# Placing the start of a long-convolution kernel by hand: Sin order, a small add, a copy, and the loads of q

## The chip, the cores and the metric

The kernel runs on one core of a Trainium2 chip. The metric is device time in microseconds (us) of one execution. Each comparison below was timed in five rounds on one chip, against fresh runs of the kernel before.

Engines are named as in the profile: PE is TensorE (matmul), DVE is VectorE, ACT is ScalarE, POOL is GpSimd, and SP is the engine whose queue issues most loads. A letter L with a number is a line of that kernel's own source, so the same statement has different numbers in different kernels.

## The reference

Shortened; only the middle lines of `_A_ref` are put in words. Shapes are 2048 rows by 576 channels, bfloat16. The program has two layers, but the reference multiplies the layernorm of x by a convolution of k and v, which does not depend on x, so the kernel computes the convolution once.

```python
def _A_ref(q, k, v, shift_k, ssm_k, ssm_D):            # q is layernorm(x)
    k_shift = sum over t of k_pad[:, t:t+S, :] * shift_k[:, ks-1-t]     # 4 taps
    kv = k_shift * v
    y = irfft(rfft(kv, zero-padded) * rfft(ssm_k, zero-padded))[:S]      # long convolution
    y = y + kv * ssm_D
    return q * y

x = A_q
x = x + _A_ref(_layernorm(x), A_k, A_v, A_shift_k, A_ssm_k, A_ssm_D)
x = x + (gelu(n @ w_gate) * (n @ w_up)) @ w_down       # n = layernorm(x)
# ... and both once more with the same inputs: the second layer
```

## The kernel before

The convolution is done by blocks of 512 rows with matrices instead of an FFT. GF is the forward transform matrix and GI the inverse one. Both are generated on the core: VectorE computes an integer angle (`j`, then `jm`), and ScalarE takes its Sin.

```python
def emit(dst, col_ap_halves, row_scalar, offs):
    j = work.tile([P, NDFT], I32, tag="dft_j", bufs=2)
    ...
    jm = work.tile([P, NDFT], I32, tag="dft_jm", bufs=3)
    nc.vector.tensor_single_scalar(out=jm[:, 0:W], in_=j[:, 0:W], scalar=N4 - 1, op=ALU.bitwise_and)
    nc.scalar.activation(out=dst, in_=jm[:, 0:W], func=ACT.Sin, bias=negpi[:], scale=sc)

for kt in range(KT_F):        # 4 pieces of GF, 128x1024
    emit(GF[:, kt, :], ...)
for kt in range(KT_I):        # 8 pieces of GI, 128x512
    emit(GI[:, kt, :], ...)
```

Then come the loads: `skb` (the four taps), `hn` (the filter, four blocks), `dvec` (ssm_D), then k and v, the first feed-forward weights, and 16 tiles of q for layernorm statistics. ScalarE rearranges the taps: `nc.scalar.copy(out=skc, in_=skb rearranged)`.

The filter blocks are transposed, copied and transformed:

```python
def fwd(src_blk, d0, dw, scale, dst):                  # 32 matmuls of dw columns, 4 evacuations
    for mt0 in range(0, MT, MP):
        ps = psT.tile([P, MP, 512], F32, tag="psT")
        ...  nc.tensor.matmul(ps[:, mi, 0:dw], lhsT=GF[...], rhs=src_blk[:, kt, d0:d0 + dw], ...)
        nc.scalar.activation(out=dst[:, mt0:mt0 + MP, :], in_=ps[:, :, 0:dw], func=ACT.Copy, scale=scale)

for blk in range(NBLK):
    hT_blk = kvp.tile([P, STB, D], BF16, tag="hT_blk")
    ...  # 20 transposes by TensorE; two ScalarE copies PSUM -> hT_blk
    if blk == 0:
        nc.vector.tensor_tensor(out=hT_blk[0:1, 0, :], in0=hT_blk[0:1, 0, :], in1=dvec[:], op=ALU.add)
    for pi in porder:                                  # 64 columns ("thin"), then 512 ("wide")
        fwd(hT_blk, d0, dw, 2.0 / NDFT, Hf[(pi, blk)])
```

An evacuation is the `activation` in `fwd`: ScalarE copies finished sums from TensorE's result buffer (`ps`) into `dst`. The same `fwd` then transforms the four kv blocks, which VectorE prepares in eight groups of multiplications and adds ("kv groups"). After that VectorE multiplies the spectra (`pr`), TensorE sums the products (`Yps`) and applies GI. From about 216 us on the feed-forward part runs, which the change does not touch.

The order of instructions on each engine is fixed when the kernel is built, by a scheduler. In the traces here an engine whose next instruction waits does not take a later one: in skb_first, below, TensorE stood 5.67 us before one matmul with 40 others behind it.

## Time and profile before

| | before |
|---|---|
| time, median of 6 runs before the prediction | 1144.62 us (1141.97 to 1147.25) |
| profiled run: time and span | 1143.58 us, 1141.8 us |
| first filter transform on TensorE | 20.52 us |
| first kv transform | 69.48 us |
| first feed-forward matmul | 215.55 us |
| feed-forward part | 926.3 us |

The page of before, parts 1 and 4: busy time of each engine, and the chain of work that ended last, by engine.

```profile
PE 1077.9 (94%) x6340; PEld 519.8 (46%) x6464; DVE 487.3 (43%) x1023; ACT 296.1 (26%) x481; POOL 47.6 (4%) x96
...
PE 82%; DVE 11%; issue 4%; ACT 2%; POOL 1%; DMA 1%; SPq 0%; DVEq 0%; POOLq 0%
```

TensorE is the limit of the whole. So a change to the other engines is worth only what it removes from TensorE's waits. The longest stands at the start. In the timeline view each line gives the start, the duration, engine, source line, operation, output<-input, shapes and count; in square brackets is how long the engine had been idle and what released it. First before's TensorE:

```profile
6.96 2.89 PE L256 MATMUL pt<-ident,hn 128*128 128x128 bf16 x20 [6.96 <-DMA hn<-in_A_ssm_k_dram]
20.52 1.01 PE L184 MATMUL ps<-hT_blk,GF 128*128 128x64 bf16 x16 [10.68 <-DVE hT_blk L260]
...
31.42 0.98 PE L256 MATMUL pt<-ident,hn 128*128 128x128 bf16 x10
```

TensorE has its transposes done at 9.85 us and then sits idle for 10.68 us. The name behind the arrow is the small `dvec` add on VectorE. The timelines of before's ScalarE and VectorE say why it is so late:

```profile
5.36 2.30 ACT L164 COPY skc<-skb 128x2304 bf16<-128x2304 bf16 x1 [3.34 <-DMA skb<-in_A_shift_k_dram]
...
9.61 1.28 ACT L58 ACT_TABLE_LOAD   x1
10.90 1.15 ACT L58 ACTIVATE GF<-jm,negpi 128x1024 bf16<-128x1024 int32 x1
11.96 1.10 ACT L258 COPY hT_blk<-pt 128x1152 bf16<-128x1152 bf16 x1
12.96 3.23 ACT L58 ACTIVATE GF<-jm,negpi 128x1024 bf16<-128x1024 int32 x3
16.09 4.51 ACT L58 ACTIVATE GI<-jm,negpi 128x512 bf16<-128x512 int32 x7
```

```profile
12.09 0.69 DVE L57 TENSOR_SCALAR jm<-j 128x1024 int32<-128x1024 int32 x1 [4.33 <-ACT GF L58]
...
19.94 0.43 DVE L260 TENSOR_TENSOR hT_blk<-hT_blk,dvec 1x576 bf16<-1x576 bf16 x1
...
22.00 0.76 DVE L274 TENSOR_TENSOR acc<-kj,skc 128x1152 bf16<-128x1152 bf16 x1 [1.22 <-DMA kj<-in_A_k_dram]
```

ScalarE's first large instruction waits for the load of the taps; behind it come a copy of `hT` (1.12 us) and the load of the Sin table (1.28 us), so the first Sin starts at 10.90 us. VectorE has only three `jm` buffers, so it waits for Sins too (4.33 us). And the add stands behind nearly all of GI's angles, though TensorE needs only GF.

### The profile page before, as it was taken

Reading aid. Unit: us, or ns where it says so; the run is one execution under the profiler, and the core shown is the slowest. Engines: PE = TensorE matmul, PEld = TensorE weight load, DVE = VectorE, ACT = ScalarE, POOL = GpSimd, SP = SyncE. Lnnn points to the kernel's source line nnn. Section 1 sums busy time; section 2 is a strip of 40 time slices with the busy share of each in tenths; the row PEclk is TensorE's granted clock in tenths of the full one; section 3 lists DMA queues with packets and bytes.
Section 4 is the critical chain, followed back from the end, with each engine's and each line's share of the span. In section 5 each row is a group of like instructions: output and inputs, shape, how many; then the busy total and the mean of one; then the engine's idle time right before and its main releaser. Section 6 shows DMA issues by size and latency. Waiting matters only on the chain.

```text
span 1141.8 us, 15444 instructions
## 1 busy us (share of the span) xinstructions
PE 1077.9 (94%) x6340; PEld 519.8 (46%) x6464; DVE 487.3 (43%) x1023; ACT 296.1 (26%) x481; POOL 47.6 (4%) x96
## 2 busy tenths in 40 slices
PE   3889888699999999999999999999999999999997
PEld 2444333344444444444444444444444444444443
DVE  6966789822256224932353236323222322232222
ACT  6555320511113111331113111311131111111111
POOL 0010000200001000200010001000000000000000
PEclk9999999899999999999999999999999999999999
DMA  8932000980000000000000000000000000000000
GB/s 248 289 99 72 1 1 3 354 265 1 1 1 1 1 1 1 1 1 1 1 1 1 1 1 1 1 1 21 1 1 1 21 1 1 1 22 1 1 1 21
DMA packets 35957, 41.09 MB, mean 36 GB/s; under 512 B 2101, under 2 KB 33712, under 8 KB 35888
## 3 DMA queue, kind: packets, MB, share of 16 engines
q1 hardware_dynamic: 33776, 35.39, 10.1%
q0 software_dynamic: 2112, 4.72, 1.5%
q8 instruction: 50, 0.82, 0.3%
q14 instruction: 19, 0.16, 0.0%
HBM read 35.38 MB, written 2.36 MB: 33 GB/s over the span
## 4 chain that ended last, share of the span: by engine, by line
PE 82%; DVE 11%; issue 4%; ACT 2%; POOL 1%; DMA 1%; SPq 0%; DVEq 0%; POOLq 0%
PE pg L506 20%; PE pu L506 20%; PE acc L523 19%; PE pu L509 5%; PE pg L509 5%; PE ps L184 4%; PE acc L526 3%; DVE pr L219 3%; PE ps L244 2%; POOL rstd L302 1%; DVE stats L298 1%; DVE x_c L315 1%; PE Yps L223 1%; PE pt L460 1%; DVE hT L517 1%
## 5 line engine op out<-in xcount | busy, mean ns | idle before, releaser
L517 DVE TENSOR_TENSOR hT<-ga,pu 128x512 bf16<-128x512 f32 x288 | 197.4, 685 | 575.8 <-PE pu L509 567.9
L515 ACT ACTIVATE ga<-pg 128x512 f32<-128x512 f32 x288 | 171.6, 596 | 685.1 <-PE pg L509 644.4
L523 PE MATMUL acc<-wd,hT 128*128 128x512 bf16 x1101 | 312.3, 380 | 2.1 <-DVE hT L517 2.1
L506 PE MATMUL pg<-xnT,wg 128*128 128x512 bf16 x1132 | 294.2, 380 | 1.2 <-issue 0.2
L506 PE MATMUL pu<-xnT,wu 128*128 128x512 bf16 x1128 | 291.6, 379 | 2.0 <-ACT ga L515 1.0
L526 PE MATMUL acc<-wd,hT 128*128 128x64 bf16 x1152 | 222.0, 193 | 2.5
L523 PEld LDWEIGHTS <-hT 128*128 128x128 bf16 x1152 | 112.7, 98 | 138.8 <-DVE hT L517 5.7
L506 PEld LDWEIGHTS <-wu 128*128 128x128 bf16 x1152 | 112.8, 98 | 137.5 <-issue 2.1
L506 PEld LDWEIGHTS <-wg 128*128 128x128 bf16 x1152 | 93.7, 98 | 102.6 <-issue 0.5
L526 PEld LDWEIGHTS <-hT 128*128 128x128 bf16 x1152 | 112.9, 98 | 32.4
L509 PE MATMUL pu<-xnT_rB,wr 128*128 128x512 bf16 x288 | 109.2, 379 | 0.9
L509 PE MATMUL pg<-xnT_rA,wr 128*128 128x512 bf16 x276 | 104.8, 380 | 0.0
L509 PEld LDWEIGHTS <-wr 128*128 128x128 bf16 x576 | 56.4, 98 | 68.1 <-issue 0.3
L219 DVE TENSOR_TENSOR pr<-KVf,Hf 128x128 bf16<-128x128 bf16 (+1 forms) x160 | 64.0, 451 | 33.3 <-PE Yps L223 16.2
L184 PEld LDWEIGHTS <-GF 128*128 128x128 bf16 x512 | 36.6, 104 | 52.4 <-issue 14.0
L184 PE MATMUL ps<-hT_blk,GF 128*128 128x64 bf16 (+1 forms) x252 | 38.6, 313 | 14.9 <-DVE hT_blk L260 10.7
L302 POOL TENSOR_TENSOR rstd<-ve,neghalf_t 128x1 f32<-128x1 f32 x48 | 35.7, 744 | 357.1 <-DVE ve L301 340.3
L223 PE MATMUL Yps<-pr,ident 128*128 128x512 bf16 (+1 forms) x176 | 44.8, 331 | 1.6 <-DVE zb L233 0.6
L298 DVE BATCH_NORM_STATS2 stats<-x_c 128x6 f32<-128x288 f32 x96 | 40.3, 437 | 0.0
L244 PE MATMUL ps<-zb,GI 128*128 128x64 bf16 (+1 forms) x190 | 29.2, 285 | 10.4 <-DVE zb L236 6.8
L440 ACT ACTIVATE xn<-x_c,nbias,rstd 128x576 bf16<-128x576 f32 x32 | 27.5, 860 | 34.9 <-DVE nbias L437 18.3
L184 PE MATMUL ps<-kv_blk,GF 128*128 128x64 bf16 (+1 forms) x253 | 32.8, 285 | 3.4 <-ACT KVf L187 1.4
(71 smaller groups left out, 449.0 us busy)
## 6 DMA issues: line engine op xcount, KB each, us to landing
kj<-in_A_k_dram SPq DMA_DIRECT2D x29, 288.0 KB, 4.3
wd<-in_B_w_down_dram SPq DMA_DIRECT2D x9, 576.0 KB, 7.2
wg<-in_B_w_gate_dram SPq DMA_DIRECT2D x9, 512.0 KB, 8.2
wu<-in_B_w_up_dram SPq DMA_DIRECT2D x9, 512.0 KB, 9.8
x_c<-in_A_q_dram POOLq DMA_DIRECT2D x4, 1152.0 KB, 7.0
v_t<-in_A_v_dram SPq DMA_DIRECT2D x8, 288.0 KB, 3.6
qt<-in_A_q_dram SPq DMA_DIRECT2D x16, 144.0 KB, 3.0
out_dram<-ob SPq DMA_DIRECT2D x16, 144.0 KB, 1.7
```

Source lines behind the costliest of these rows:

```text
L184: nc.tensor.matmul(ps[:, mi, 0:dw], lhsT=GF[:, kt, mt * P:(mt + 1) * P], rhs=src_blk[:, kt, d0:d0 + dw], start=(kt == 0), stop=(kt == KT_F ...
L219: nc.vector.tensor_tensor(out=pr[:], in0=kvf[:, ko:ko + HH, :], in1=hf[:, ho:ho + HH, :], op=ALU.mult)
L223: nc.tensor.matmul(Yflat[:, c0:c0 + cw], lhsT=idm[:], rhs=prf[:, c0:c0 + cw], start=(ti == 0), stop=(ti == n_terms - 1))
L244: nc.tensor.matmul(ps[:, mi, 0:dw], lhsT=GI[:, kt, mt * P:(mt + 1) * P], rhs=zb[:, kt, :], start=(kt == 0), stop=(kt == KT_I - 1))
L298: nc.vector.bn_stats(out=stats[:, h, :], in_=x_ap[:, h * w:(h + 1) * w])
L302: nc.gpsimd.tensor_tensor(out=rstd_out, in0=ve[:], in1=neghalf_t[:, 0:1], op=ALU.pow)
L506: nc.tensor.matmul(pd[:], lhsT=wm[:, dt, fi * P:(fi + 1) * P], rhs=xnT[:, dt, :], start=(dt == 0), stop=(dt == NDTF - 1 and not DREM))
L509: nc.tensor.matmul(pd[:], lhsT=wr[g][:, fi * P:(fi + 1) * P], rhs=rr[:], start=False, stop=True)
L515: nc.scalar.activation(out=ga[:], in_=pg[:], func=ACT.Gelu_apprx_tanh)
L517: nc.vector.tensor_tensor(out=hT[:], in0=ga[:], in1=pu[:], op=ALU.mult)
L523: nc.tensor.matmul(acc[:, j, 0:DM], lhsT=hT[:, j * P:(j + 1) * P], rhs=wd[g][:, fi, 0:DM], start=(f == 0), stop=(f == FT - 1))
L526: nc.tensor.matmul(acc[:, STC, j * DR:(j + 1) * DR], lhsT=hT[:, j * P:(j + 1) * P], rhs=wd[g][:, fi, DM:D], start=(f == 0 and j == 0), sto ...
```

## The change

The intent is to let TensorE's first transform start earlier, without new work. Most of it is ordering: dependencies that only the scheduler sees, and that add no wait on the chip. No arithmetic is added or removed.

- The four GF pieces go first on VectorE and ScalarE; the index row `colf` is made before the identity matrix on POOL.
- The `dvec` add goes before GI; the tap copy goes behind the four thin evacuations of block 0; the eight GI Sins go between wide evacuations (three in block 0, five in block 1).
- The q loads move from SP's queue to POOL's, with two buffers instead of three, and the q statistics come behind kv block 0.
- The first down-projection weight is loaded after the convolution part.

The core of the diff, with cuts marked by dots:

```diff
+        colf = tmpc.tile([P, NF], F32, name="colf")
+        nc.gpsimd.iota(colf[:], ...)          # before ident and rowf
+        if pre_cb is not None:
+            pre_cb()                          # make_identity
...
+    i_skc = nc.scalar.copy(out=skc[:], in_=skb[:].rearrange("p d j -> p j d"))
+    after(i_skc, "gf_last_sin", "DMA-fed rearrangement must not block the DFT matrix generation")
...
-            nc.scalar.copy(out=hT_blk[:, j0:j0 + MP, :], in_=pt[:, :, 0:D])
+            i_cp = nc.scalar.copy(out=hT_blk[:, j0:j0 + MP, :], in_=pt[:, :, 0:D])
+            if blk == 0:
+                after(i_cp, "gf_last_sin", "GF first on ScalarE")
         if blk == 0:
-            nc.vector.tensor_tensor(out=hT_blk[0:1, 0, :], ..., in1=dvec[:], op=ALU.add)
+            i_add = nc.vector.tensor_tensor(out=hT_blk[0:1, 0, :], ..., in1=dvec[:], op=ALU.add)
+            for i_gi in marks["gi_ands"]:
+                tc.add_manual_dep(i_gi.ins, i_add.ins.name, SCHED, reason="dvec add before GI")
...
+    sched(i_skc, evac[3], "skc behind the thin evacuations of block 0")
+    for i in range(8):
+        sched(marks["gi_sins"][i], evac[4 + i if i < 3 else 8 + i], "GI Sins between wide evacuations")
...
+                    if g == 0:
+                        after(i_first, "gf_last_and", "GF first on VectorE (kv ops wait on DMA)")
+                        tc.add_manual_dep(i_first.ins, i_add.ins.name, SCHED, reason="dvec add first")
+                        sched(i_first, marks["gi_ands"][2], "3 GI pieces before the kv ops")
...
+        if blk == 0 and early_cb is not None:
+            early_cb[1](ktmp, lambda inst: tc.add_manual_dep(inst.ins, i_kvlast.ins.name, SCHED,
+                                                             reason="q stats after kv block 0"))
...
-            qt = scratch.tile([P, D], BF16, tag="qtmp", bufs=3)
-            nc.sync.dma_start(out=qt[:], in_=q2[st * P:(st + 1) * P, :])
+            qt = scratch.tile([P, D], BF16, tag="qtmp", bufs=2)
+            nc.gpsimd.dma_start(out=qt[:], in_=q2[st * P:(st + 1) * P, :])
...
+    alloc_w(wpool, 0, gu=False)
+    load_w(0, gu=False)                       # wd of group 0, now behind the convolution part
```

More of the change, by code (lines that the diff above doesn't have):

```diff
@@ L21, with _gen_dft_mats @@
 NF = BS
-def _gen_dft_mats(tc, pool_gf, pool_gi, G_dtype, tmpc, work):
+def _gen_dft_mats(tc, pool_gf, pool_gi, G_dtype, tmpc, work, pre_cb=None):
     nc = tc.nc
@@ L30, in _gen_dft_mats @@
     GI = pool_gi.tile([P, KT_I, BS], G_dtype, name="GI")
+    marks = {}
     if True:
@@ L34, in _gen_dft_mats @@
                        allow_small_or_imprecise_dtypes=True)
+        colf = tmpc.tile([P, NF], F32, name="colf")
+        nc.gpsimd.iota(colf[:], pattern=[[2, NF]], base=1, channel_multiplier=0,
+                       allow_small_or_imprecise_dtypes=True)
+        if pre_cb is not None:
+            pre_cb()
         rowf = tmpc.tile([P, 2, KT_F], F32, name="rowf")
         nc.gpsimd.iota(rowf[:], pattern=[[0, 2], [2 * P, KT_F]], base=1, channel_multiplier=2,
-                       allow_small_or_imprecise_dtypes=True)
-        colf = tmpc.tile([P, NF], F32, name="colf")
-        nc.gpsimd.iota(colf[:], pattern=[[2, NF]], base=1, channel_multiplier=0,
                        allow_small_or_imprecise_dtypes=True)
@@ L56, in emit @@
             jm = work.tile([P, NDFT], I32, tag="dft_jm", bufs=3)
-            nc.vector.tensor_single_scalar(out=jm[:, 0:W], in_=j[:, 0:W], scalar=N4 - 1, op=ALU.bitwise_and)
-            nc.scalar.activation(out=dst, in_=jm[:, 0:W], func=ACT.Sin, bias=negpi[:], scale=sc)
+            i_and = nc.vector.tensor_single_scalar(out=jm[:, 0:W], in_=j[:, 0:W], scalar=N4 - 1, op=ALU.bitwise_and)
+            i_sin = nc.scalar.activation(out=dst, in_=jm[:, 0:W], func=ACT.Sin, bias=negpi[:], scale=sc)
+            return i_and, i_sin
         for kt in range(KT_F):
-            emit(GF[:, kt, :], [(colf[:], NF), (colf[:], NF)], rowv[:, kt:kt + 1],
-                 [3 * NDFT, 0])
+            i_and, i_sin = emit(GF[:, kt, :], [(colf[:], NF), (colf[:], NF)], rowv[:, kt:kt + 1],
+                                [3 * NDFT, 0])
+        marks["gf_last_and"] = i_and
+        marks["gf_last_sin"] = i_sin
         for kt in range(KT_I):
             off = 3 * NDFT if kt < KT_F else 0
-            emit(GI[:, kt, :], [(colt[:], BS)], rowf[:, kt // KT_F, kt % KT_F: kt % KT_F + 1], [off])
-    return GF, GI
+            i_and, i_sin = emit(GI[:, kt, :], [(colt[:], BS)], rowf[:, kt // KT_F, kt % KT_F: kt % KT_F + 1], [off])
+            marks.setdefault("gi_sins", []).append(i_sin)
+            marks.setdefault("gi_ands", []).append(i_and)
+        marks["gi_last_and"] = i_and
+        marks["gi_last_sin"] = i_sin
+    return GF, GI, marks
 @with_exitstack
 def ssm_phase_A(ctx, tc, y_sb, ident, A_k, A_v, A_shift_k, A_ssm_k, A_ssm_D, G_dtype=BF16,
-                after_loads_cb=None, early_cb=None):
+                after_loads_cb=None, early_cb=None, pre_cb=None):
     nc = tc.nc
@@ L110, in ssm_phase_A, with after @@
     dft_work = dft_es.enter_context(tc.tile_pool(name="dft_work", bufs=2))
-    GF, GI = _gen_dft_mats(tc, gfp, gip, G_dtype, dft_tmp, dft_work)
+    GF, GI, marks = _gen_dft_mats(tc, gfp, gip, G_dtype, dft_tmp, dft_work, pre_cb=pre_cb)
+    SCHED = mybir.DependencyInfo(mybir.DependencyClass.NoSync, mybir.DependencyReason.SCHED_ONLY)
+    def after(inst, mark, why):
+        tc.add_manual_dep(inst.ins, marks[mark].ins.name, SCHED, reason=why)
     hn = []
@@ L149, in ssm_phase_A @@
             else:
-                nc.vector.memset(kj[0:j, 0, :], 0.0)
+                i_ms = nc.vector.memset(kj[0:j, 0, :], 0.0)
+                after(i_ms, "gf_last_and", "GF first on VectorE")
                 nc.sync.dma_start(out=kj[j:P, 0, :], in_=k2[0:P - j, :])
@@ L157, in ssm_phase_A @@
         ksh_all.append((ksh, v_t))
-        if g == 1 and after_loads_cb is not None:
-            after_loads_cb()
-    if early_cb is not None:
-        early_cb(dft_work)
+        if g == 1:
+            if after_loads_cb is not None:
+                after_loads_cb()
+            if early_cb is not None:
+                early_cb[0](ktmp)
     dft_es.close()
-    nc.scalar.copy(out=skc[:], in_=skb[:].rearrange("p d j -> p j d"))
+    i_skc = nc.scalar.copy(out=skc[:], in_=skb[:].rearrange("p d j -> p j d"))
+    after(i_skc, "gf_last_sin", "DMA-fed rearrangement must not block the DFT matrix generation")
     sgn_i = gip.tile([P, 1], I32, name="sgn_i")
@@ L176, in ssm_phase_A @@
     MP = 2
+    evac = []
     def fwd(src_blk, d0, dw, scale, dst):
@@ L186, in fwd @@
                                      start=(kt == 0), stop=(kt == KT_F - 1))
-            nc.scalar.activation(out=dst[:, mt0:mt0 + MP, :], in_=ps[:, :, 0:dw], func=ACT.Copy, scale=scale)
+            evac.append(nc.scalar.activation(out=dst[:, mt0:mt0 + MP, :], in_=ps[:, :, 0:dw], func=ACT.Copy, scale=scale))
     ypool_cm = tc.tile_pool(name="A_Y", bufs=1)
@@ L257, in ssm_phase_A @@
                                         identity=ident[0:dsz, 0:dsz])
-            nc.scalar.copy(out=hT_blk[:, j0:j0 + MP, :], in_=pt[:, :, 0:D])
+            i_cp = nc.scalar.copy(out=hT_blk[:, j0:j0 + MP, :], in_=pt[:, :, 0:D])
+            if blk == 0:
+                after(i_cp, "gf_last_sin", "GF first on ScalarE")
         if blk == 0:
-            nc.vector.tensor_tensor(out=hT_blk[0:1, 0, :], in0=hT_blk[0:1, 0, :], in1=dvec[:], op=ALU.add)
+            i_add = nc.vector.tensor_tensor(out=hT_blk[0:1, 0, :], in0=hT_blk[0:1, 0, :], in1=dvec[:], op=ALU.add)
+            for i_gi in marks["gi_ands"]:
+                tc.add_manual_dep(i_gi.ins, i_add.ins.name, SCHED, reason="dvec add before GI")
         for pi in porder:
@@ L263, in ssm_phase_A, with sched @@
             fwd(hT_blk, d0, dw, 2.0 / NDFT, Hf[(pi, blk)])
+    def sched(a, b, why):
+        tc.add_manual_dep(a.ins, b.ins.name, SCHED, reason=why)
+    sched(i_skc, evac[3], "skc behind the thin evacuations of block 0")
+    for i in range(8):
+        sched(marks["gi_sins"][i], evac[4 + i if i < 3 else 8 + i], "GI Sins between wide evacuations")
     for blk in range(NBLK):
@@ L273, in ssm_phase_A @@
                 if idx == 0:
-                    nc.vector.tensor_tensor(out=acc[:], in0=ksh[j][:], in1=skj, op=ALU.mult)
+                    i_first = nc.vector.tensor_tensor(out=acc[:], in0=ksh[j][:], in1=skj, op=ALU.mult)
+                    if g == 0:
+                        after(i_first, "gf_last_and", "GF first on VectorE (kv ops wait on DMA)")
+                        tc.add_manual_dep(i_first.ins, i_add.ins.name, SCHED, reason="dvec add first")
+                        sched(i_first, marks["gi_ands"][2], "3 GI pieces before the kv ops")
                 else:
@@ L278, in ssm_phase_A @@
                     nc.vector.tensor_tensor(out=acc[:], in0=acc[:], in1=tmp[:], op=ALU.add)
-            nc.vector.tensor_tensor(out=kv_blk[:, gi * GST:(gi + 1) * GST, :], in0=acc[:], in1=v_t[:], op=ALU.mult)
+            i_kvlast = nc.vector.tensor_tensor(out=kv_blk[:, gi * GST:(gi + 1) * GST, :], in0=acc[:], in1=v_t[:],
+                                               op=ALU.mult)
+            if g == 0:
+                for i in range(3, 8):
+                    sched(marks["gi_ands"][i], i_kvlast, "rest of GI after kv group 0")
         for pi in porder:
@@ L346, in ssm_geglu_kernel @@
     ident = persist.tile([P, P], BF16, name="ident")
-    make_identity(nc, ident[:])
     eps_t = persist.tile([P, 1], F32, name="eps_t")
@@ L354, in ssm_geglu_kernel, with alloc_w @@
     fw = FG * P
-    def alloc_w(pool, g):
-        wg[g] = pool.tile([P, NDTF, fw], BF16, name=f"wg{g}")
-        wu[g] = pool.tile([P, NDTF, fw], BF16, name=f"wu{g}")
-        wr[g] = pool.tile([P, fw], BF16, name=f"wr{g}") if DREM else None
-        wd[g] = pool.tile([P, FG, D], BF16, name=f"wd{g}")
-    def load_w(g):
-        f0 = g * fw
-        nc.sync.dma_start(out=wg[g][:], in_=B_w_gate[0:NDTF * P, f0:f0 + fw].rearrange("(dt p) f -> p dt f", p=P))
-        nc.sync.dma_start(out=wu[g][:], in_=B_w_up[0:NDTF * P, f0:f0 + fw].rearrange("(dt p) f -> p dt f", p=P))
-        if DREM:
-            nc.sync.dma_start(out=wr[g][0:DREM, :], in_=B_w_gate[NDTF * P:D, f0:f0 + fw])
-            nc.sync.dma_start(out=wr[g][DREM:2 * DREM, :], in_=B_w_up[NDTF * P:D, f0:f0 + fw])
-        nc.sync.dma_start(out=wd[g][:], in_=B_w_down[f0:f0 + fw, :].rearrange("(ft p) d -> p ft d", p=P))
+    def alloc_w(pool, g, gu=True, dn=True):
+        if gu:
+            wg[g] = pool.tile([P, NDTF, fw], BF16, name=f"wg{g}")
+            wu[g] = pool.tile([P, NDTF, fw], BF16, name=f"wu{g}")
+            wr[g] = pool.tile([P, fw], BF16, name=f"wr{g}") if DREM else None
+        if dn:
+            wd[g] = pool.tile([P, FG, D], BF16, name=f"wd{g}")
@@ new lines, in load_w @@
+    def load_w(g, gu=True, dn=True):
+        f0 = g * fw
+        if gu:
+            nc.sync.dma_start(out=wg[g][:], in_=B_w_gate[0:NDTF * P, f0:f0 + fw].rearrange("(dt p) f -> p dt f", p=P))
+            nc.sync.dma_start(out=wu[g][:], in_=B_w_up[0:NDTF * P, f0:f0 + fw].rearrange("(dt p) f -> p dt f", p=P))
+            if DREM:
+                nc.sync.dma_start(out=wr[g][0:DREM, :], in_=B_w_gate[NDTF * P:D, f0:f0 + fw])
+                nc.sync.dma_start(out=wr[g][DREM:2 * DREM, :], in_=B_w_up[NDTF * P:D, f0:f0 + fw])
+        if dn:
+            nc.sync.dma_start(out=wd[g][:], in_=B_w_down[f0:f0 + fw, :].rearrange("(ft p) d -> p ft d", p=P))
@@ L371, in ssm_geglu_kernel, with q_loads @@
     pre = ctx.enter_context(tc.tile_pool(name="pre", bufs=1))
-    alloc_w(pre, 0)
+    alloc_w(pre, 0, dn=False)
     qmv = persist.tile([P, NST, 2], F32, name="qmv")
     qrstd = persist.tile([P, NST], F32, name="qrstd")
-    def q_stats(scratch):
+    q_tiles = []
+    def q_loads(scratch):
+        for st in range(NST):
+            qt = scratch.tile([P, D], BF16, tag="qtmp", bufs=2)
+            nc.gpsimd.dma_start(out=qt[:], in_=q2[st * P:(st + 1) * P, :])
+            q_tiles.append(qt)
@@ L378, in q_stats, with q_compute @@
+    def q_compute(scratch, after_fn):
         nchunk = 2 if D > nc.vector.BN_STATS_FMAX else 1
@@ L380, in q_stats @@
         for st in range(NST):
-            qt = scratch.tile([P, D], BF16, tag="qtmp", bufs=3)
-            nc.sync.dma_start(out=qt[:], in_=q2[st * P:(st + 1) * P, :])
+            qt = q_tiles[st]
             stats = scratch.tile([P, nchunk, nc.vector.BN_STATS_DIM], F32, tag="qstats", bufs=2)
             for h in range(nchunk):
-                nc.vector.bn_stats(out=stats[:, h, :], in_=qt[:, h * w:(h + 1) * w])
+                i_bn = nc.vector.bn_stats(out=stats[:, h, :], in_=qt[:, h * w:(h + 1) * w])
+                if h == 0:
+                    after_fn(i_bn)
             nc.vector.bn_aggr(out=qmv[:, st, :], in_=stats[:])
@@ L389, in q_stats @@
         nc.gpsimd.tensor_tensor(out=qrstd[:], in0=ve[:], in1=neghalf_t[:, 0:1].to_broadcast([P, NST]), op=ALU.pow)
-    ssm_phase_A(tc, y_sb, ident, A_k, A_v, A_shift_k, A_ssm_k, A_ssm_D, after_loads_cb=lambda: load_w(0),
-                early_cb=q_stats)
+    ssm_phase_A(tc, y_sb, ident, A_k, A_v, A_shift_k, A_ssm_k, A_ssm_D, after_loads_cb=lambda: load_w(0, dn=False),
+                early_cb=(q_loads, q_compute), pre_cb=lambda: make_identity(nc, ident[:]))
     if debug == "y":
```

## The prediction

> **What bounds the kernel now.** TensorE: the page has PE busy 94% of 1141.8 us, and the chain of waits is 82% PE. From 217 us on runs the feed-forward part, which the change does not touch. The change works on the first 110 us (making the DFT matrices GF and GI by Sin, block transforms of the filter, then of kv) and on when some loads are issued.
>
> **Where time is lost there.** In the timeline PE finishes its first transposes at 9.85 us and waits 10.7 us for the first transform (20.5). Its last releaser is the dvec add (19.94 us, 0.43 us), which stands behind nearly all of GI's generation on VectorE. Behind that: ScalarE waits until 5.36 us for the skb load, copies it (2.30 us), copies hT (1.12 us), and only then starts the Sins at 10.9 us.
>
> **What the change does.** No arithmetic goes. The four GF Sins (1.15 us each) go before everything fed by a load; the dvec add before GI; the eight GI Sins (0.72 us) between evacuations; the skb copy behind the thin evacuations. The q loads move from SP's queue to POOL's with two buffers instead of three, q statistics behind kv block 0, and the first down-projection weight is loaded after the SSM phase.
>
> **New start, from the trace's durations.** colf ready about 1.5 us; one GF piece each 1.4 us on VectorE; identity 2.5, then its negation and a table load (1.28) to about 4.2; four Sins end at about 8.7. The hn load (6.9 us) and transposes (9.85) now gate: hT copies end at about 11. dvec is issued near 4.7 us instead of 8.7, behind three hn blocks; at the 300 GB/s of the windows it lands near 10.5. Add 0.43: first transform at about 11.6 us, **8.9 us earlier**.
>
> **How much survives.** A wide evacuation (1.02 us) comes every 1.73 us, so one Sin just fits between two. The Sin behind block 1's last evacuation delays the next hT copies: −0.7 us. PE's cold stretch (half-rate spacing until 26.4 us) may shorten a little: the Trainium skill, "TensorE: Matmul & The Clock Gate", Part 1, describes warming after sustained activity; this trace shows about 6 us of it. VectorE must reach the first products by about 68 us on the new scale; summing its work I get 64, so 4 us of slack. q tiles through POOL (the skill's "DMA: Bandwidth & Descriptors", Anatomy of one DMA, gives that path about 2 us fixed cost; here SP's took 3.0) may stall VectorE 0 to 7 us in all, mostly inside this slack: −0.5 expected. The late weight is needed 17 us after its issue; such loads land in 7 to 9: no cost.
>
> **Prediction: 1136.8 us**, range 1132.5 to 1141.5: about −8 us (0.7%). Chances: faster by over 2% 0.02, within 2% 0.97, slower 0.01.
>
> **What would show it.** Right: first transform matmul at 11 to 13 us; first kv transform (69.5 us before) and first feed-forward matmul (215.5) about 8 us earlier; feed-forward length unchanged at about 926 us. Wrong: first transform past 14 us; VectorE waiting on q loads for more than 4 us; evacuations waiting on a Sin that waits for VectorE; PE idle more than 1 us before kv blocks 2 and 3.
>
> **What would make it wrong.** Stalls behind the q loads, passed on through VectorE's fixed order to the kv blocks, could give back up to 5 us. PE dropping to half rate at other block boundaries moves the result about 1.7 us each way. Later stages, where VectorE and PE alternate, may realign and swallow or add some us.

## The result, and the profile after

The changed kernel took 1135.38 us (median of 8 runs, 1134.43 to 1136.46) against 1145.18 us (median of 16 runs, 1141.97 to 1147.25) for before, whose six runs from before the prediction are counted too. The ratio is 0.9919, with an interval of 0.9909 to 0.9928. A ratio here is the mean time of one kernel's runs over that of the other's of the same rounds, so it is not quite the ratio of the medians. Run again later, unaltered, beside the last experiments, it took 1137.38 us (5 runs, 1136.28 to 1137.74), ratio 0.9935 (0.9922 to 0.9947). So the gain is 7 to 10 us, and the predicted 1136.8 us lies between the two medians.

After's page, the same two lines:

```profile
PE 1079.5 (95%) x6340; PEld 519.7 (46%) x6464; DVE 486.1 (43%) x1023; ACT 295.9 (26%) x481; POOL 58.0 (5%) x112
...
PE 82%; DVE 10%; issue 4%; POOL 1%; ACT 1%; DMA 1%; SPq 0%; DVEq 0%; POOLq 0%
```

No work went. POOL has 16 more instructions, the q loads, and 10 us more busy time. The timeline of after's TensorE, ScalarE and VectorE:

```profile
11.14 2.48 PE L203 MATMUL ps<-hT_blk,GF 128*128 128x64 bf16 x33 [1.51 <-DVE hT_blk L281]
...
21.46 0.98 PE L275 MATMUL pt<-ident,hn 128*128 128x128 bf16 x10
```

```profile
3.25 1.28 ACT L61 ACT_TABLE_LOAD   x1
4.54 3.23 ACT L61 ACTIVATE GF<-jm,negpi 128x1024 bf16<-128x1024 int32 x3
7.98 1.15 ACT L61 ACTIVATE GF<-jm,negpi 128x1024 bf16<-128x1024 int32 x1 [0.21 <-DVE jm L60]
9.04 2.12 ACT L277 COPY hT_blk<-pt 128x1152 bf16<-128x1152 bf16 x2
...
13.32 2.24 ACT L180 COPY skc<-skb 128x2304 bf16<-128x2304 bf16 x1
16.48 1.02 ACT L206 ACTIVATE Hf<-ps 128x1024 bf16<-128x1024 f32 x1 [0.93 <-PE ps L203]
17.41 0.71 ACT L61 ACTIVATE GI<-jm,negpi 128x512 bf16<-128x512 int32 x1
18.21 1.02 ACT L206 ACTIVATE Hf<-ps 128x1024 bf16<-128x1024 f32 x1
```

```profile
10.65 0.45 DVE L281 TENSOR_TENSOR hT_blk<-hT_blk,dvec 1x576 bf16<-1x576 bf16 x1 [1.49 <-DMA dvec<-in_A_ssm_D_dram]
...
20.35 0.76 DVE L303 TENSOR_TENSOR acc<-kj,skc 128x1152 bf16<-128x1152 bf16 x1 [6.58 <-DMA kj<-in_A_k_dram]
...
68.54 1.10 DVE L238 TENSOR_TENSOR pr<-KVf,Hf 128x128 bf16<-128x128 bf16 x4
...
70.96 1.29 DVE L238 TENSOR_TENSOR pr<-KVf,Hf 128x1024 bf16<-128x1024 bf16 x2 [1.32 <-ACT KVf L206]
```

The first transform starts 9.38 us earlier. TensorE's wait fell from 10.68 to 1.51 us, and its last releaser is now a load, `dvec`, that lands a little before 10.65 us. That load is issued at 4.78 us instead of 8.67. In before, SP's queue held it behind the load of the fourth filter block, whose buffer the taps occupied until the tap copy ended at 7.66 us; in after it goes ahead of that load (22.01 us). The GI Sins slip between wide evacuations as intended (16.48, 17.41, 18.21).

How the gain travelled, in us from the start of the span, read from the TensorE timelines. B1 to B3 are the first transposes of filter blocks 1 to 3, kv0 and kv3 the first matmuls of kv blocks 0 and 3. The dips are explained below the table. The last three rows are runs that are told further down.

| kernel | first transform | B1 | B2 | B3 | kv0 | kv3 | feed-forward | span | dips |
|---|---|---|---|---|---|---|---|---|---|
| before | 20.52 | 31.42 | 43.25 | 56.24 | 69.48 | 98.01 | 215.55 | 1141.8 | 3 |
| after | 11.14 | 21.46 | 34.96 | 48.76 | 62.26 | 90.80 | 208.50 | 1134.8 | 4 |
| after, run again | 11.29 | 21.95 | 33.77 | 47.05 | 60.22 | 90.33 | 209.99 | 1136.0 | 4 |
| ffn_q | 11.21 | 21.30 | 33.12 | 48.17 | 61.67 | 90.22 | 207.34 | 1135.0 | 4 |
| ffn_q_fill | 11.17 | 21.92 | 33.84 | 46.11 | 58.02 | 86.57 | 203.63 | 1132.1 | 1.6 |

A dip is a stretch in which the granted TensorE clock falls to half. I found them by reading the clock in windows of 2 us from 22 to 200 us and adding up what was missing from 1.00. In before that sum is 5.14 us, in after 6.84, in its second run 6.80: 3, 4 and 4 times 1.71 us. So each dip is about 3.4 us at half rate and costs at most 1.71 us. All 14 profiled runs have one longer half-rate stretch outside this count, around the first feed-forward matmul: 200.47 to 210.71 us in after. In ffn_q_fill it begins before 200 us, which makes the 0.6. The windows view shows one dip, which begins just ahead of the wide matmuls of block 1. Its columns are the window, its length, busy time and instruction count of PE, PEld, DVE, ACT and POOL, then the granted clock, the DMA share and GB/s. First after, then the same kernel's second run:

```profile
25.00:28.00 3.00, 2.51 (x33) 1.48 (x34) 2.97 (x7) 1.74 (x5) 0.00 (x0) 0.73 1.08 321
28.00:31.00 3.00, 3.00 (x11) 1.21 (x10) 2.93 (x6) 1.02 (x2) 0.00 (x0) 0.70 1.09 377
```

```profile
25.00:28.00 3.00, 2.33 (x36) 1.54 (x36) 2.93 (x7) 2.08 (x6) 0.00 (x0) 1.00 1.10 313
28.00:31.00 3.00, 3.00 (x16) 1.35 (x15) 2.94 (x6) 2.12 (x3) 0.00 (x0) 1.00 1.06 348
```

It is the same program at the same place. Once there is a dip (0.73 and 0.70: 0.81 + 0.90 = 1.71 us missing) and 11 wide matmuls fit in 3 us; once there is none and 16 fit. Block 1 took 13.50 us from its transposes to block 2's in the one run and 11.82 in the other. Before's profiled run had no dip there (11.83). So the same program does both: this is chance of the run and not a fixed effect of the change. Windows of 0.1 us show what is regular in it. In each profiled run all half-rate stretches start on one grid of 3.41 us and last one to four steps of it: in after they start at 26.39, 40.04, 53.70, 166.34 and 200.47 us, that is 4, 4, 33 and 10 steps apart. The grid lies elsewhere in each run. In after the step before the first dip (22.98 to 26.39 us) holds 2.16 us of busy TensorE; in the second run the step at this place (23.81 to 27.22 us) holds 2.16 us as well, and no dip follows. So what decides is not the busy time alone, and stays open.

The two profiled spans have to be compared with that in mind: 1141.8 − 1134.8 = 7.0 us, with one dip more in after; 8.7 us at equal dips, if every dip cost its full 1.71. The timed runs, which average over such chances, say 9.8 us in the first rounds and 7.1 us in the later ones.

### The profile page after: what moved, and what is told of

Read it like the earlier page. It is cut to its first block, busy times and chain, and to the rows that moved or that the text cites. A ratio compares the mean times of both kernels' runs of the same rounds, so it can differ in the third digit from the quotient of the medians.

```text
span 1134.8 us, 15449 instructions
## 1 busy us (share of the span) xinstructions
PE 1079.5 (95%) x6340; PEld 519.7 (46%) x6464; DVE 486.1 (43%) x1023; ACT 295.9 (26%) x481; POOL 58.0 (5%) x112
## 4 chain that ended last, share of the span: by engine, by line
PE 82%; DVE 10%; issue 4%; POOL 1%; ACT 1%; DMA 1%; SPq 0%; DVEq 0%; POOLq 0%
PE pg L560 20%; PE pu L560 20%; PE acc L577 20%; PE pu L563 5%; PE pg L563 5%; PE ps L203 5%; PE acc L580 3%; DVE pr L238 3%; PE ps L263 2%; POOL rstd L342 1%; DVE stats L338 1%; DVE x_c L355 1%; PE Yps L242 1%; DVE hT L571 1%; PE pt L512 1%
```

## The experiments

Theory A is that of the prediction: the whole gain is the earlier first transform. TensorE is the limit from there to the kv blocks, so a microsecond won at 11 us is a microsecond at the end. Rivals: the gain comes from the moved q loads, which free SP's queue (B); a part of the possible gain is lost again, to TensorE's half-rate stretches (C) or to VectorE arriving late behind q statistics and loads (D).

Twelve runs were made, one of them (after_again) of after itself, in three groups of four on three chips, each against before on its own chip. All gave correct results. Across groups only the ratios are to be compared.

| run | median us (runs) | before | ratio (interval) |
|---|---|---|---|
| start_only | 1137.75 (5) | 1145.47 | 0.9934 (0.9921 to 0.9946) |
| q_only | 1144.40 (5) | 1145.47 | 0.9990 (0.9977 to 1.0002) |
| gi_first | 1140.83 (5) | 1145.47 | 0.9961 (0.9948 to 0.9973) |
| skb_first | 1146.98 (5) | 1145.47 | 1.0019 (1.0005 to 1.0032) |
| fill_b1 | 1137.12 (5) | 1144.36 | 0.9939 (0.9924 to 0.9954) |
| fill_all | 1138.62 (5) | 1144.36 | 0.9945 (0.9932 to 0.9957) |
| late_q | 1141.28 (6) | 1144.36 | 0.9965 (0.9949 to 0.9981) |
| late_q_fill | 1135.25 (4) | 1144.36 | 0.9916 (0.9903 to 0.9930) |
| after_again | 1137.38 (5) | 1144.48 | 0.9935 (0.9922 to 0.9947) |
| ffn_q | 1136.39 (5) | 1144.48 | 0.9928 (0.9915 to 0.9940) |
| ffn_q_fill | 1133.64 (4) | 1144.48 | 0.9905 (0.9892 to 0.9919) |
| ffn_q_fill_start | 1134.09 (4) | 1144.48 | 0.9908 (0.9893 to 0.9923) |

### The two halves of the change: start_only and q_only

start_only is after with the q loads, q statistics and down-projection weight put back:

```diff
-            qt = scratch.tile([P, D], BF16, tag="qtmp", bufs=2)
-            nc.gpsimd.dma_start(out=qt[:], in_=q2[st * P:(st + 1) * P, :])
+            qt = scratch.tile([P, D], BF16, tag="qtmp", bufs=3)
+            nc.sync.dma_start(out=qt[:], in_=q2[st * P:(st + 1) * P, :])
...
-    alloc_w(wpool, 0, gu=False)
-    load_w(0, gu=False)
```

> The start's new order alone; q loads, q statistics and the first down-projection weight as in the kernel before. Theory A (the gain is the earlier first transform): first transform at 11 to 12 us as in the changed kernel, time 1135 to 1137.5 us, so 80 to 100% of the gain. Theory B (the gain needs the q loads and the weight off the SP queue): above 1140 us.

q_only is before with those parts alone changed, in the opposite direction, and the order at the start left as it was.

> The q loads, q statistics and late weight alone, start order as before. Theory A: first transform still at about 20.5 us and time 1144 to 1146 us, no gain. Theory B: below 1140 us.

Measured: start_only has a ratio of 0.9934, slightly outside what was expected in microseconds, with the first transform at 10.67 us. q_only has 0.9990 and its first transform at 20.68 us. So theory A holds and B falls: the start carries the gain, and the q part alone shows none. What the q part adds on top of the new start is not resolved by time, since after itself gave 0.9919 once and 0.9935 once. The trace of start_only does show one thing that the q part avoids. Its timelines of VectorE, ScalarE and TensorE, in that order:

```profile
34.64 0.82 DVE L425 BATCH_NORM_STATS2 stats<-qt 128x6 f32<-128x288 bf16 x2 [3.21 <-DMA qt<-in_A_q_dram]
...
37.28 0.72 ACT L61 ACTIVATE GI<-jm,negpi 128x512 bf16<-128x512 int32 x1 [1.24 <-DVE jm L60]
...
39.06 0.22 PE L203 MATMUL ps<-hT_blk,GF 128*128 128x64 bf16 x2 [1.99 <-ACT hT_blk L277]
```

VectorE stood 3.21 us behind a q load, so the angle for the last GI Sin came late; ScalarE waited for it with the copies of block 2 behind it, and TensorE waited 1.99 us (0.64 us at this place in after, at 37.85 us). A load that nothing urgent needs had reached TensorE through two other engines' fixed order.

### Two halves of the start: gi_first and skb_first

gi_first is after with the `dvec` add behind GI's angles again and the GI Sins not placed:

```diff
-            for i_gi in marks["gi_ands"]:
-                tc.add_manual_dep(i_gi.ins, i_add.ins.name, SCHED, reason="dvec add before GI")
+            tc.add_manual_dep(i_add.ins, marks["gi_last_and"].ins.name, SCHED, reason="dvec add behind GI")
...
-    for i in range(8):
-        sched(marks["gi_sins"][i], evac[4 + i if i < 3 else 8 + i], "GI Sins between wide evacuations")
...
-            if g == 0:
-                for i in range(3, 8):
-                    sched(marks["gi_ands"][i], i_kvlast, "rest of GI after kv group 0")
```

> The changed kernel with only GI put back before the dvec add (on VectorE and with its Sins unplaced on ScalarE); GF still first. Theory A (both the early Sins and the early dvec add are needed): first transform at 16 to 18 us, time 1140 to 1142.5 us. Rival (ScalarE's wait for skb was the whole of it): first transform below 13 us, under 1137 us.

Measured: 1140.83 us, as expected. The first two matmuls started at 14.70, the rest at 16.15 us, and about half of the gain was gone. The last cut of the edit, which frees five of the GI angles from their place behind kv group 0, was not tried alone.

skb_first is after with ScalarE's start as before: the tap copy ahead of the Sins, and the copies of `hT` where the scheduler likes.

```diff
-    after(i_skc, "gf_last_sin", "DMA-fed rearrangement must not block the DFT matrix generation")
...
-            if blk == 0:
-                after(i_cp, "gf_last_sin", "GF first on ScalarE")
...
-    sched(i_skc, evac[3], "skc behind the thin evacuations of block 0")
+    tc.add_manual_dep(marks["gf_first_sin"].ins, i_skc.ins.name, SCHED, reason="skb copy first, as before")
```

> The changed kernel with only ScalarE's start put back (skb copy and a hT copy before the GF Sins); dvec add still before GI. Theory A: GF's last Sin ends near 15 us, first transform at 16 to 17.5 us, time 1140 to 1142 us. Rival (the dvec add's place was the whole of it): first transform below 13 us, under 1137 us.

Measured: 1146.98 us, a miss by about 5 us, and slower than before although the first transforms ran at 13.10 and 15.48 us. The start was a little earlier than expected: kv block 0 was reached at 65.05 us, 4.4 us before before's. The loss came behind it, in the timeline of skb_first's TensorE:

```profile
66.33 0.63 PE L203 MATMUL ps<-kv_blk,GF 128*128 128x64 bf16 x16 [0.88 <-ACT Hf L206]
72.62 0.27 PE L242 MATMUL Yps<-pr,ident 128*128 128x128 bf16 x1 [5.67 <-DVE pr L238]
```

The scheduler had put one product matmul into the middle of kv block 0. VectorE, which had q statistics to do first, delivered its product 5.67 us after TensorE wanted it, and the other 40 transform matmuls of the block stood behind it. The granted clock was at half from 69.00 to 75.82 us as well, so the first of them ran at half rate. So an earlier start is worth nothing if the order further on makes TensorE meet VectorE too early. This named the second limit that D proposes.

### Half-rate stretches: fill_b1 and fill_all

Both are after, with six matmuls of 512 columns whose result nobody reads behind the transposes of a block, so that TensorE stays busy while ScalarE copies `hT`. fill_b1 has them in block 1 alone, fill_all in blocks 1 to 3:

```diff
+        if blk == 1:            # fill_all: blk > 0
+            fps = psY.tile([P, HH, 512], F32, tag="Yps", name="fps")
+            for fi in range(6):
+                i_f = nc.tensor.matmul(fps[:, fi % HH, :], lhsT=GF[:, 0, 0:P], rhs=GF[:, 1, 0:512],
+                                       start=True, stop=True)
+                tc.add_manual_dep(i_f.ins, i_tp.ins.name, SCHED, reason="filler behind the transposes")
```

> The changed kernel plus six idle-time matmuls of 512 columns, read by nobody, behind the transposes of block 1, where TensorE waits for the hT copies. Theory C (TensorE's clock falls to half after the thin stretch at a block boundary, and eight wide matmuls at 0.43 instead of 0.22 us cost 1.7 us): granted clock 1.0 in the window where it was 0.56 (26 to 29 us), block 1 from transposes to next transposes 11.8 instead of 13.5 us; later blocks unchanged. In time only 1 to 1.7 us come out (1133.7 to 1134.4), as VectorE has 1.3 us of slack before the first products. Rival D (evacuations and Sins set the block's length): block 1 stays 13.5 us or grows by the fillers' 1.3 us.

> The same fillers at blocks 1, 2 and 3. Theory C with VectorE next: each block about 11.8 us, kv block 0 starts 4 to 5 us earlier than in the changed kernel (57 to 58.5 us), but VectorE reaches the first products at about 68 us as before, TensorE waits for it, and the time falls by 2 us or less (1133.4 to 1135). If VectorE were not next: 1130 to 1131.5. Rival D: no block gets shorter.

Measured: block 1 took 11.91 us in fill_b1, without a dip, as theory C expected. But the unaltered kernel did as well in its second run (11.82), so this single block shows nothing. fill_all says more: it had no dip at all between 22 and 62 us, where after had three, and reached kv block 0 at 58.26 us, 4.0 us before after's first run. Yet neither gained time: the ratios are 0.9939 and 0.9945, against after's 0.9919 and 0.9935, and both are misses. In fill_all's timeline TensorE now waits for VectorE, at two places of kv block 1:

```profile
69.67 0.22 PE L242 MATMUL Yps<-pr,ident 128*128 128x128 bf16 x1 [1.84 <-DVE pr L238]
...
72.55 0.22 PE L242 MATMUL Yps<-pr,negident 128*128 128x128 bf16 x1 [1.93 <-DVE pr L238]
```

The 4 us were handed to VectorE as waiting time. The second run of after shows the same at a smaller scale. It came to kv block 0 two microseconds earlier than the first run, and its timeline has:

```profile
72.64 0.22 PE L242 MATMUL Yps<-pr,negident 128*128 128x128 bf16 x1 [1.35 <-DVE pr L238]
...
81.95 0.22 PE L242 MATMUL Yps<-pr,ident 128*128 128x128 bf16 x1 [1.55 <-DVE pr L238]
```

It kept 0.47 of its 2.04 us at kv block 3. So C is right about the cause and wrong about its worth: in after, a dip in the filter blocks costs little, since VectorE would have been the next to wait for.

### Moving VectorE's work: late_q and late_q_fill

late_q is after with the second half of the q statistics behind the last kv group instead of behind kv block 0, and the first product matmul held behind kv block 0's transform. late_q_fill adds the fillers of fill_all.

```diff
-        if blk == 0 and early_cb is not None:
+        if blk in (0, NBLK - 1) and early_cb is not None:
             early_cb[1](ktmp, lambda inst: tc.add_manual_dep(inst.ins, i_kvlast.ins.name, SCHED, ...),
+                        range(8) if blk == 0 else range(8, NST), blk > 0)
```

> The changed kernel with the statistics of q tiles 8 to 15 moved behind the last kv group (no fillers). VectorE reaches the first products about 7 us earlier and waits there. As TensorE is the slower of the two in the changed kernel by 1.3 us, no gain: 1134.5 to 1136.5. If VectorE was already the limit: below 1133.5.

> Both: fillers at blocks 1 to 3 and half of the q statistics late. Theory C with VectorE next: the gain that neither brings alone: 1130 to 1132 us. If the fillers' gain is lost elsewhere: above 1133.

Measured: both missed. late_q took 1141.28 us. It reached kv block 3 at 90.26 us, but from there to the feed-forward part it took 122.2 us instead of after's 117.7, with two dips in this stage where after had one, and with this in its timeline of TensorE:

```profile
104.97 1.01 PE L244 MATMUL Yps<-pr,ident 128*128 128x512 bf16 x2 [2.76 <-DVE pr L240]
```

The late statistics, waiting for their own loads, now stood in front of the products. That is not the whole loss: two of the six runs took 1138.01 us at a mean granted clock of 0.989, the other four 1140.89 to 1142.60 us at 0.986, so 3 to 4 us of it come and go with the clock. late_q_fill, at 1135.25 us (ratio 0.9916), won 4.1 us at kv block 3 and gave part of it back in the same stage. Where VectorE's work is put matters as much as how much it is.

### Taking it away: after_again, ffn_q, ffn_q_fill, ffn_q_fill_start

In the second layer the feed-forward part computes the gate's statistics itself, in chunks. ffn_q lets it do so in the first layer too for 12 of the 16 tiles, where VectorE is 25 to 54% busy in the four stretches that I read (after, 217 to 640 us). Only the first four tiles, which the first chunk needs, stay in the convolution part. The first product matmul is held behind kv block 0, so TensorE's order of instructions is exactly that of after.

```diff
-        for st in range(NST):          # q loads and q statistics
+        for st in range(STC):          # 4 tiles
...
-   ...append(lambda j=j, ncu=ncu: gate_A1_st(ncu * STC + j, layer0=True))
+   ...append(lambda j=j, ncu=ncu: gate_A1_st(ncu * STC + j))
```

ffn_q_fill adds the fillers of fill_all. ffn_q_fill_start adds to that two fp32 matmuls at the very start and three fillers behind block 0's transposes. after_again is the unaltered changed kernel, for comparison on the same chip.

> The changed kernel once more, unaltered, as the reference on this chip. Expected: ratio to before 0.991 to 0.993, profiled span 1134 to 1136 us, first transform at 11.1 us. If the half-rate stretch in block 1 follows from the order of work, block 1 takes 13.5 us from its first transpose to block 2's again; if it is chance, it may take 11.9 us this time.

> The changed kernel with 12 of the 16 tiles of q statistics taken out of the convolution part; the first layer's feed-forward part computes them itself, as the second layer's does. TensorE's order is the same, VectorE has about 13 us less to do before the products. Theory A (TensorE and ScalarE pace the transforms, VectorE has slack in the changed kernel): nothing gained, kv block 3 at 90.8 us again, ratio 0.991 to 0.993. Rival (the q statistics and their loads cost the changed kernel 2 us or more): ratio 0.990 or less, kv block 3 at 89 us or earlier.

> The same as ffn_q, with six throw-away matmuls behind the transposes of blocks 1 to 3. With them alone VectorE had become the limit at kv blocks 1 and 2; with its load cut, the 4 us that the fillers win should arrive: kv block 3 at 86.7 us, first feed-forward matmul at 204.3 to 205.5, span 1131 to 1132.5, ratio 0.988 to 0.990. If it is no better than the changed kernel (0.991 or more), something other than VectorE takes the gain: the middle stage growing, or a feed-forward part that starts at a lower rate.

> The same as ffn_q_fill, with two fp32 throw-away matmuls of the column numbers at the very start and three behind block 0's transposes, so that TensorE may be warm when its first transform starts. If warmth comes of dense activity before, the half-rate stretch of block 0 (5.3 us in the changed kernel) shrinks to 3 us or less: kv block 3 at 84.5 to 86 us, ratio 0.986 to 0.988. If the fillers delay the transposes as much as they save, the ratio is that of ffn_q_fill.

Measured: after_again is told above; its ratio of 0.9935 is just outside what was expected, and 11.8 us in block 1 says that the dip there was chance.

ffn_q has a ratio of 0.9928 and kv block 3 at 90.22 us: nothing gained that can be told from after_again's 0.9935, so the q statistics cost the changed kernel no 2 us, as theory A expected.

ffn_q_fill took 1133.64 us. Its four runs (1132.87 to 1134.90) all lie below after_again's five (1136.28 to 1137.74), and 1133.64 against 1137.38 us is 3.7 us less. The ratio 0.9905 is just above the expected 0.988 to 0.990. It and ffn_q_fill_start, which differs little from it (1134.05 to 1134.21 us), are the versions that beat both kernels on the same chip. Fillers alone had gained nothing and less VectorE work alone had gained nothing that shows; together they gain. Its timeline of TensorE:

```profile
68.47 0.63 PE L205 MATMUL ps<-kv_blk,GF 128*128 128x64 bf16 x16 [0.71 <-ACT KVf L208]
...
78.19 0.22 PE L244 MATMUL Yps<-pr,ident 128*128 128x128 bf16 x1 [1.25 <-DVE pr L240]
...
86.57 0.34 PE L205 MATMUL ps<-kv_blk,GF 128*128 128x64 bf16 x6 [0.21 <-DVE kv_blk L323]
```

The waits of fill_all are gone from kv block 1. From kv block 0 to kv block 3 it takes 28.55 us, as after does (28.54), where after_again took 30.11. And it has no dip in blocks 1 to 3; these are its windows of blocks 1 and 2:

```profile
25.00:28.00 3.00, 2.74 (x40) 1.73 (x39) 2.93 (x7) 1.97 (x6) 0.00 (x0) 1.00 1.10 314
28.00:31.00 3.00, 3.00 (x15) 1.37 (x14) 2.93 (x6) 2.05 (x3) 0.00 (x0) 1.00 1.09 371
37.00:40.00 3.00, 2.54 (x39) 1.61 (x37) 2.49 (x6) 1.72 (x5) 0.36 (x1) 1.00 0.90 272
40.00:43.00 3.00, 3.00 (x16) 1.36 (x14) 2.85 (x8) 1.17 (x2) 0.28 (x1) 1.00 0.39 114
```

All four kernels with fillers in blocks 1 to 3 (fill_all, late_q_fill, and the two here) had no dip between 22 and 62 us. All ten profiled runs without them there had one to three. That the fillers prevent them in these blocks is therefore shown by more than one chance.

ffn_q_fill lost some of its 4.9 us at the feed-forward part, which took 928.5 us instead of 926.3. No run was made to test what makes up these 2 us, but the traces divide them. Every version begins this part at half rate: after for 2.2 us (208.50 to 210.71), ffn_q_fill for 4.6 us (203.63 to 208.20), where its first two groups of four wide matmuls took 1.91 us each instead of 1.03. At half rate the 2.4 us more cost about 1.2 us, an estimate. About 1 us is left, and it shows in ffn_q (927.7 us, 3.0 us at half rate) and ffn_q_fill_start (927.8 us, 2.95 us) too. These three do 12 tiles of statistics there that were done before, now on 32-bit data; that this is the cause is likely and not tested.

ffn_q_fill_start missed its expectation: a ratio of 0.9908, kv block 3 at 86.10 us. Its fillers did shorten the half-rate stretch of block 0. Counting matmuls in 2 us shows it, first in after, then in ffn_q_fill_start:

```profile
14.00:16.00 2.00, 2.00 (x6) 0.60 (x5) 0.00 (x0) 1.56 (x1) 0.00 (x0) 1.00 0.79 232
16.00:18.00 2.00, 2.00 (x10) 0.92 (x9) 0.00 (x0) 1.51 (x2) 0.00 (x0) 1.00 0.59 206
```

```profile
14.00:16.00 2.00, 2.00 (x11) 0.91 (x10) 0.01 (x1) 2.00 (x2) 0.00 (x0) 1.00 0.67 173
```

Six wide matmuls fit where eleven fit at full rate. It reached block 1 at 20.19 us, 1.7 us before ffn_q_fill, and was only 0.47 us ahead at kv block 0. Its blocks 1 and 2 took 12.50 and 12.94 us without a dip, so something other than the clock held them. I see GI Sins between evacuations that now come faster, and ScalarE waiting 0.55 us for an angle with block 2's copies behind it (at 34.47 us); how much of the loss that makes was not tested.

## Why the prediction was right

**The time.** Predicted were 1136.8 us (1132.5 to 1141.5), within 2%. Measured were 1135.38 and, in the later rounds, 1137.38 us. The signs "about 8 us earlier" came out near it: the first kv transform was 7.22 us earlier in after and 9.26 us in its second run, the first feed-forward matmul 7.05 and 5.56 us.

**"First transform at about 11.6 us, 8.9 us earlier": right, by its mechanism.** It came at 11.14 and 11.29 us. Gain: 9.38 us, so the term was 0.5 us too small. The two releasers that the prediction put close together are there: the `hT` copies ended at 11.16 us (predicted: about 11), and the `dvec` add ran at 10.65 us when its load, issued at 4.78 us (predicted: near 4.7), had landed. Estimating a load's landing from its place in the queue and the bytes ahead of it was good to a few tenths. start_only and q_only show that this is the whole of the resolved gain.

**"The Sin behind block 1's last evacuation delays the next hT copies: −0.7": right.** In after, TensorE's second batch of transposes of block 2 starts at 36.24 us and the first transform at 37.85, a gap of 1.61 us against 1.01 in block 1 and in before's block 2. So 0.6 us for the first two matmuls, and 0.4 us for the rest of them (2.63 us behind these transposes, 2.19 in before).

**"PE's cold stretch may shorten a little": right.** The first wide evacuation moved from 26.25 to 16.48 us, by 9.77 us, 0.4 us more than the start.

**"q tiles through POOL may stall VectorE 0 to 7 us in all, mostly inside this slack": right in size.** The stall was 3.1 us, seven times at most 0.8, against 2.3 us in before. No cost is seen in after; ffn_q, which removes three quarters of the tiles and has 1.24 us of this stall left, gains nothing resolved. The Trainium skill, "DMA: Bandwidth & Descriptors", Anatomy of one DMA, gives about 2.0 us plus bytes over 436 KB per us for that path, which would make 2.3 us for a tile of 144 KB, an estimate; the pages of before and after give 3.0 us median through either queue, and the measured figure is the one to use.

**"VectorE must reach the first products by about 68 us; summing its work I get 64": wrong by 4.5 us.** It reached them at 68.54 us. The parts of the sum are not on record, so what it left out is not shown. The largest wait that a sum of work misses is that of kv group 0 for k: 6.58 us (until 20.35 us), where the same wait in before was 1.22 us, because VectorE got there earlier. The slack was not 4 us but 1.3: in after, VectorE then waited 1.3 us for an evacuation of kv block 0. In the first run TensorE's dips kept it slow enough for this not to matter. In the second run TensorE was 2 us quicker at kv block 0, and VectorE took 1.6 us of it back. So the nearness of 1136.8 is partly luck, by an estimate from these figures: the start and the cold stretch gave 0.9 us more than predicted, while one dip more (1.7 us, first run) or VectorE (1.6 us, second run) took more than the 0.5 us set aside for stalls. A sum of busy times is a lower bound; the loads have to be put into it.

**"The late weight: no cost", "feed-forward length unchanged at about 926 us": right.** The first down-projection matmul comes 5.35 us after the first feed-forward matmul in before and 5.41 us in after; the feed-forward part took 926.3 us in both.

**"PE dropping to half rate at other block boundaries moves the result about 1.7 us each way": right in size per dip (1.71 us), too narrow in number.** The ten profiled runs without fillers in all three blocks had from three to five dips between 22 and 200 us. That before's own 16 runs spread by 5.3 us fits this. Only profiled executions were looked at for dips, but the mean granted clock is on record for the 29 runs of before beside the experiments: the eight at 0.990 took 1142.84 to 1144.25 us, the 21 at 0.987 to 0.989 took 1144.31 to 1147.29 us. The profiled difference of 7.0 us and the timed ones of 9.8 and 7.1 us should not be read to a tenth.

**"PE idle more than 1 us before kv blocks 2 and 3"** was named as a sign of being wrong, and by its letter it appeared: TensorE waited 1.25 us for a product near the start of kv block 2. It is not a loss: kv block 0 to kv block 3 took 28.53 us in before and 28.54 in after, and ffn_q, whose VectorE had far less to do, has the same wait (1.26 us).

## What to carry to other kernels

Follow the limiting engine's first long wait back through each other engine's fixed order, and ask of every instruction in front of the one it waits for whether it is needed yet: here a copy fed by a load and half of a table stood in front, and moving them was worth 0.6 to 0.8%. After such a move the next engine's slack is what matters; sum its work including the loads it will now be early for, because two changes that each gained nothing (fillers, less VectorE work) gained 3.7 us together. And run an unaltered kernel a second time before reading meaning into one profiled difference of a microsecond or two.

## What the Trainium skill lacked or had wrong

- "TensorE: Matmul & The Clock Gate", Part 1: its table has the half rate come back after an idle window of about 3.4 us. Here it came back after windows that were not idle. In the 3.41 us before after's first dip (22.98 to 26.39 us) TensorE was busy 2.16 us by the profile, with 42 mostly thin matmuls and two short waits; in ffn_q the window before the dip at 165.93 us was busy for 3.15 us. The same part tells further on of a kernel in which short idles between groups of matmuls were enough, without a measure. It lacks what thin matmuls count for, and that a few wide throw-away matmuls in such a place prevent the drop (no dip in four of four kernels, one to three in ten of ten runs without).
- The same part: a free-running window of 3.4 us agrees with the runs here, in which all half-rate stretches of one execution lie on one grid of 3.41 us (four of its steps are 13.65 us in after, from 26.39 to 40.04 us). It says that the number of cold matmuls varies from run to run and costs under 1%. That is so, and it lacks the consequence for tuning: one dip more or less is 1.7 us here, a fifth of the gain studied.
- The same part: warm-up after about 3.4 us of sustained activity. In after the half rate lasted from 11.14 us to about 16.3 us, with 2.5 us of thin matmuls at its beginning; in before from 20.52 to about 26.4 us. That is longer than 3.4 us, but both ends lie on the grid of later dips carried back (16.15 and 26.47 us), so it agrees with a window that has to be filled from its beginning. The profile's granted clock reads 1.00 in this first stretch (windows of 14 to 16 us above), so it has to be seen from the number of matmuls instead.
- "DMA: Bandwidth & Descriptors", Anatomy of one DMA: its fit would give 2.3 us for a 144 KB load through POOL, an estimate; the median was 3.0 us, the same as through SP. Other loads were under way (DMA share 0.88 and 0.70 in after from 37 to 43 us), so the fit for a single load is not refuted.
- "ScalarE: Activation LUTs", What ACT_TABLE_LOAD costs: 1283 ns for the load agrees (1.28 us at 3.25 us in after). The further 1380 ns of drain do not show: the instruction before ended at 3.23 us and the first Sin started at 4.54 us.
